# Durations and landing times of loads and crossbar transposes in a build-time instruction scheduler, changed

## The chip, the cores and the metric

The kernel runs on one core of one Trainium2 chip. The metric is the device time of one execution in microseconds (us). Every execution quoted here was in the fast state, with a granted TensorE clock of 0.993 to 1.000 of full speed. Ratios are the mean time of one kernel's fast runs over that of the other's of the same rounds, so they are not quite the ratios of the medians quoted beside them; intervals are 95%.

## The reference

Causal attention for 8 batches of 8 heads, 576 tokens of width 64, with 16 "beacon" keys and values in front that every token may see; then a two-layer MLP (512 to 2048 to 512) with a squared ReLU over all 4,608 tokens.

```python
k_all = np.concatenate([beacon_k, k], axis=2)          # B=8, H=8, 16+576, 64
v_all = np.concatenate([beacon_v, v], axis=2)
scores = scale * np.matmul(q, k_all.transpose(0, 1, 3, 2))
scores = np.where(causal, -1e9, scores)
a = softmax(scores)                                     # cut
x = np.matmul(a, v_all).transpose(0, 2, 1, 3).reshape(4608, 512)
r = np.maximum(x @ w_in, 0.0)
return (r * r) @ w_out
```

## The kernel before

The program is not written in its final order. The Python code adds some 1,360 operations, each with a guessed duration, a priority and what it depends on; a small event simulation ("the model") then plays them, and each engine's instructions are emitted in the order in which the model started them. The model's clock is never on the chip: what is frozen into the program is only the order. On the chip each engine takes its instructions in that order and waits, by semaphore, for whatever is not ready.

All DMAs share one modelled stream, `dma_free`; each adds its `dma` to it:

```python
# Order.run(): an operation starts on engine e at model time `now`
end = now + dur
free[e] = end
if op.dma:
    dma_free = max(dma_free, now + self.DMA_LAT[e]) + op.dma
    seen = max(end, dma_free + 1.6)          # model time at which its users may start
    lanes[e].append(seen)
    ...
else:
    seen = end + self.LAT[e]
```

The three kinds of DMA that the change touches:

```python
# add_load(): 128 rows of q, k or v of one batch, fp32, into a staging buffer; POOL casts it to bf16
ld = add(f"ld{b}{x}{c}", "POOL" if soft else "SP", 1.3 if lo else 0.65, emit_load, prio=prio, take=("stg", "stg"),
         dma=(1.15 if b < NPE else 1.25) * rows / 128, behind=load_chain[-1:] + behind, sync=sync)

# add_trans(): DMA transpose of a whole batch's q or k into qT or kT (batches 2 to 7; TensorE does batches 0 and 1)
trans[b, x] = [add(f"tr{b}{x}", "SP", 4.1, emit, prio=prio, deps=deps, dma=4.5)]

# add_first_loads(): the first 240 tokens of batch 0: head pair 0, pair 1, pairs 2-3; k on SP's queue, q on ACT's
for lo, hi in ((0, 1), (1, 2), (2, HP)):
    for n, (x, t) in enumerate((("k", k), ("q", q))):
        ... # emit: dma_start on (nc.sync, nc.scalar)[n]
        o = add(f"fld{x}{lo}", ("SP", "ACT")[n], (0.45, 0.55)[n], emit, prio=-300.0 + lo, dma=0.68 * (hi - lo))
```

In the middle of the run TensorE has two kinds of work to mix: attention of batch b, which needs loads and transposes that arrive by DMA, and MLP matmuls of earlier tokens, which need nothing from DMA. A good order puts attention where its data has landed and MLP everywhere else.

The softmax here doesn't subtract the row's maximum and nothing guards it: scores larger than these inputs give would overflow.

## Time and profile before

The median is 346.06 us at first (346.27 with the run taken beside the changed kernel). From the page of the profile of the kernel before, the span, PE's (TensorE's) line of the busy times, and the busy tenths of PE and DMA in 40 slices of 8.6 us:

```profile
span 345.0 us, 7128 instructions
...
PE 327.1 (95%) x2829; PEld 174.0 (50%) x2868; DVE 168.4 (49%) x372; ACT 194.7 (56%) x297; POOL 90.7 (26%) x141
...
PE   2799899999998999999999999999999999999995
...
DMA  9999969999999999998699979984014011011002
```

TensorE bounds the kernel: it is busy 95% of the span. DMA is nearly full until about 230 us and then hardly used: in that time attention's data arrives, and from 260 us on there is MLP work alone. (39 matmul records are missing from this trace: 2829 of 2868.)

What TensorE waited for in the kernel before (the view of waits: who waited for whom, then us in total, times, longest us; the view leaves out the shortest gaps, its smallest entries are 0.2 us):

```profile
PE ps L451 <- DVE qk_area L299: 6.4, 3, 4.0
PE ps L639 <- POOL vb L299: 2.9, 4, 1.2
PE strip L589 <- ACT pt L604: 1.0, 4, 0.4
...
PE strip L589 <- DVE kT L299: 0.5, 1, 0.5
```

The first line is the startup. The second is the attention's second product, which waits for casts of v; the last two times are these, in PE's timeline (start us, us, engine, line, operation, tiles, shape, count, and in brackets the idle time before it and what ended it):

```profile
107.34 0.45 PE L639 MATMUL ps<-vb,pt 128*128 128x65 bf16 x9
108.35 0.31 PE L639 MATMUL ps<-vb,pt 128*128 128x65 bf16 x5 [0.57 <-POOL vb L299]
109.44 0.19 PE L639 MATMUL ps<-vb,pt 80*128 80x65 bf16 x1 [0.78 <-POOL vb L299]
109.69 0.59 PE L770 MATMUL ps<-xT,w_in 128*128 128x512 bf16 x2
```

MLP matmuls (L770) were ready but stood behind it in the order. Last, VectorE (DVE) in the startup of the kernel before:

```profile
4.86 0.41 DVE L299 COPY kT<-ps 128x240 bf16<-128x240 bf16 x1
6.16 0.32 DVE L299 CAST qk_area<-osb 120x256 bf16<-120x256 f32 x1 [0.89 <-DMA osb<-in_k_dram]
6.40 0.17 DVE L299 COPY kT<-ps 128x64 bf16<-128x64 bf16 x1
7.16 0.41 DVE L299 COPY kT<-ps 128x240 bf16<-128x240 bf16 x1 [0.58 <-PE ps L451]
7.76 0.63 DVE L299 CAST qk_area<-osb 120x256 bf16<-120x256 f32 x2 [0.20 <-DMA osb<-in_q_dram]
8.75 0.42 DVE L614 TENSOR_TENSOR pt<-pt,tri 128x512 bf16<-128x512 bf16 x1 [0.36 <-ACT pt L604]
9.10 0.87 DVE L299 CAST qk_area<-osb 120x256 bf16<-120x256 f32 x2
```

The cast at 6.16 waits for head pair 1's k, and the beacon copy at 6.40, which the very first scores need, stands behind it.

### The profile page before, as it was taken

To read this page: it belongs to the slowest core of one execution; us is meant where nothing else is said; L and a number is where in the kernel's file an instruction comes from. 1 tells how busy PE (TensorE), PEld (TensorE's weight loads), DVE (VectorE), ACT (ScalarE), POOL (GpSimd) and SP (SyncE) were. 2 spreads that over 40 slices of the span, in tenths; PEclk is the share of its full clock that TensorE was granted. 3 is DMA by queue.
4 is the path that set the end of the run, shared out by engine and by line. 5 is a ranking of instruction groups with operands and counts; after the bars stand their busy time and mean duration, and the time that the engine had idled before them with its cause. 6 is when DMAs were issued, how large, how long until landed. Compare 5 with 4: busy or idle time off the path is not lost.

```text
span 345.0 us, 7128 instructions
## 1 busy us (share of the span) xinstructions
PE 327.1 (95%) x2829; PEld 174.0 (50%) x2868; DVE 168.4 (49%) x372; ACT 194.7 (56%) x297; POOL 90.7 (26%) x141
## 2 busy tenths in 40 slices
PE   2799899999998999999999999999999999999995
PEld 1567675544553444444456855544554444444442
DVE  5888884158534873575355546457533302401400
ACT  4796674377645764576656655577536416515611
POOL 9844703316414504250153115312000000000000
PEclk9999999999999999999999999999999999999999
DMA  9999969999999999998699979984014011011002
GB/s 169 220 206 220 205 101 209 214 240 211 177 219 198 232 182 170 209 221 176 142 256 207 178 148 208 228 204 101 2 64 128 0 61 63 0 61 64 0 21 101
DMA packets 145291, 51.88 MB, mean 150 GB/s; under 512 B 132458, under 2 KB 140010, under 8 KB 145258
## 3 DMA queue, kind: packets, MB, share of 16 engines
q1 hardware_dynamic: 135741, 42.45, 61.4%
q0 software_dynamic: 8512, 8.49, 14.5%
q10 hardware_dynamic: 1005, 0.49, 0.6%
q8 instruction: 22, 0.36, 0.5%
q14 instruction: 11, 0.09, 0.1%
HBM read 37.22 MB, written 9.44 MB: 135 GB/s over the span
## 4 chain that ended last, share of the span: by engine, by line
PE 78%; DMA 11%; SPq 3%; ACT 3%; POOL 2%; issue 1%; DVE 1%; DVEq 0%; ACTq 0%; POOLq 0%
PE ps L805 32%; PE ps L770 31%; PE ps L639 7%; DMA stg<-in_v_dram 6%; PE strip L589 6%; ACT pt L604 2%; DMA stg<-in_k_dram 2%; DMA stg<-in_q_dram 1%; DMA osb<-in_k_dram 1%; SPq L344 1%; SPq L376 1%; POOL vb L299 1%; POOL qk_area L299 1%; PE ps L451 1%; PE ps L707 0%
## 5 line engine op out<-in xcount | busy, mean ns | idle before, releaser
L770 PE MATMUL ps<-xT,w_in 128*128 128x512 bf16 (+3 forms) x690 | 133.2, 340 | 0.6
L805 PE MATMUL ps<-w_out,g 128*128 128x512 bf16 x551 | 131.2, 379 | 1.9 <-issue 0.8
L604 ACT ACTIVATE pt<-strip 128x832 bf16<-128x832 f32 (+4 forms) x128 | 103.6, 867 | 38.4 <-PE strip L589 38.2
L786 ACT ACTIVATE g<-ps 128x512 bf16<-128x512 f32 (+2 forms) x128 | 72.0, 562 | 47.9 <-PE ps L770 47.4
L770 PEld LDWEIGHTS <-w_in 128*128 128x128 bf16 x704 | 65.2, 98 | 57.6 <-issue 6.5
L795 DVE TENSOR_TENSOR g<-g 128x1024 bf16<-128x1024 bf16 (+2 forms) x80 | 52.4, 659 | 76.5 <-ACT g L786 75.3
L805 PEld LDWEIGHTS <-g 128*128 128x128 bf16 x576 | 52.5, 98 | 60.0 <-issue 3.2
L299 POOL CAST qk_area<-stg 128x512 bf16<-128x512 f32 (+2 forms) x60 | 39.3, 662 | 53.2 <-DMA stg<-in_k_dram 31.8
L299 POOL CAST vb<-stg 128x512 bf16<-128x512 f32 (+1 forms) x38 | 26.2, 697 | 87.4 <-DMA stg<-in_v_dram 83.0
L297 ACT COPY osb<-ps 128x512 f32<-128x512 f32 x26 | 15.2, 586 | 50.8 <-PE ps L805 44.5
L639 PEld LDWEIGHTS <-pt 128*128 128x128 bf16 (+1 forms) x960 | 36.4, 98 | 14.7 <-issue 3.4
L639 PE MATMUL ps<-vb,pt 128*128 128x65 bf16 (+1 forms) x960 | 40.3, 194 | 3.0 <-POOL vb L299 2.9
L589 PE MATMUL strip<-qT,kT 64*128 64x80 bf16 (+7 forms) x400 | 36.0, 283 | 2.2 <-ACT pt L604 1.0
L659 DVE TENSOR_TENSOR xn<-ps,rcp 128x320 bf16<-128x320 f32 (+2 forms) x64 | 31.5, 492 | 2.4 <-DVE rcp L657 0.2
L614 DVE TENSOR_TENSOR pt<-pt,tri 128x1024 bf16<-128x1024 bf16 (+1 forms) x36 | 23.6, 656 | 13.4 <-ACT pt L604 13.4
L657 DVE RECIPROCAL rcp<-ps 128x5 f32<-128x5 f32 (+2 forms) x64 | 12.3, 192 | 34.6 <-PE ps L639 34.4
L788 DVE TENSOR_SCALAR g<-ps 128x512 bf16<-128x512 f32 (+2 forms) x32 | 19.1, 599 | 9.9 <-PE ps L770 9.2
L589 PEld LDWEIGHTS <-kT 64*128 64x128 bf16 x400 | 12.8, 95 | 21.6 <-issue 17.0
L299 DVE COPY osb<-ps 128x512 f32<-128x512 f32 x10 | 6.9, 692 | 14.9 <-PE ps L805 14.6
L618 DVE TENSOR_TENSOR pt<-pt,tri 80x160 bf16<-80x160 bf16 x32 | 11.5, 359 | 0.0
L344 POOL DMA_DIRECT2D stg<-in_v_dram x10 | 8.5, 854 | 6.9 <-DMA w_in<-in_moe_w_in_dram 5.5
L451 PE MATMUL ps<-ident,qk_area 120*128 120x120 bf16 x16 | 2.5, 299 | 6.5 <-DVE qk_area L299 6.4
(39 smaller groups left out, 68.6 us busy)
## 6 DMA issues: line engine op xcount, KB each, us to landing
out_dram<-osb SPq DMA_DIRECT2D x17, 512.0 KB, 3.7
stg<-in_q_dram SPq DMA_DIRECT2D x24, 256.0 KB, 4.9
stg<-in_k_dram SPq DMA_DIRECT2D x18, 256.0 KB, 5.2
stg<-in_v_dram SPq DMA_DIRECT2D x18, 256.0 KB, 4.7
w_in<-in_moe_w_in_dram POOLq DMA_DIRECT2D x4, 512.0 KB, 11.1
w_out<-in_moe_w_out_dram POOLq DMA_DIRECT2D x4, 512.0 KB, 11.6
stg<-in_v_dram POOLq DMA_DIRECT2D x6, 256.0 KB, 8.4
stg<-in_k_dram SPq DMA_DIRECT2D x6, 224.0 KB, 4.2
```

Of the source, the lines that this page charges most:

```text
L297: nc.scalar.copy(dst, src)
L299: eng[e].tensor_copy(dst, src)
L589: nc.tensor.matmul(st[:, hj, at:at + t1 - t0], kT[b % 2][hp, pr, 128 * c:128 * c + 128], qT[b % 2][hp, pr, t0:t1], start=True, stop=True,)
L604: nc.scalar.activation(pt[take_pt.held[2]][:, :, off:off + width], st[:, :, 0:width], AF.Exp, bias=0.0, scale=scale)
L614: nc.vector.tensor_tensor(out=d, in0=d, in1=tri[:, m0:m0 + m, :][:, None].to_broadcast([128, 2, m, 128]), op=ALU.min)
L639: nc.tensor.matmul(a[:, at + (t - tl[0]) * (D + 1):at + (t - tl[0] + 1) * (D + 1)], P[0:rr, hj, o:o + 128], vb[b % 2][0:rr, c, 2 * pr + hj ...
L659: nc.vector.tensor_tensor(out=xn[b % 2].rearrange("p t (h d) -> p h t d", d=D)[:, h0:h0 + nh, tl[0]:tl[0] + nt], in0=a[:, :, :, 0:D], in1= ...
L770: nc.tensor.matmul(h[:, lo - spans[0][0]:hi - spans[0][0]], w_in_sb[:, mc, ft * 128:(ft + 1) * 128], xT[:, mc, lo % RING:lo % RING + hi - lo],
L786: nc.scalar.activation(dst, h, AF.Relu, bias=0.0, scale=1.0)
L788: nc.vector.tensor_scalar(out=dst, in0=h, scalar1=0.0, scalar2=None, op0=ALU.max)
L795: nc.vector.tensor_tensor(out=d, in0=d, in1=d, op=ALU.mult)
L805: nc.tensor.matmul(o, G[:, fc, ts * 128:(ts + 1) * 128], w_out_sb[:, fc, :], start=(fc == 0), stop=(fc == NFT - 1))
```

## The change

Its likely intent is to give the model what a trace shows: the first loads in their real landing order, v loads and crossbar transposes seen later than the stream alone would say, transposes that hold the stream for 3.7 us instead of 4.5, and batch 1's beacon keys out of the startup. No operation is added or removed; a few copies and casts come out on another engine (ACT has 6 instructions fewer, DVE 5 and POOL 1 more), as the model gives them to whichever engine is free.

```diff
-                 gate=None, dma=0.0, pe_time=0.0, behind=(), sync=()):
+                 gate=None, dma=0.0, pe_time=0.0, behind=(), sync=(), late=0.0):
@@ Order.run
                         lanes[e].append(seen)
+                        seen += op.late
@@ add_load
-                 prio=prio, take=("stg", "stg"), dma=(1.15 if b < NPE else 1.25) * rows / 128, behind=..., sync=sync)
+                 prio=prio, take=("stg", "stg"), dma=(1.15 if b < NPE else 1.25) * rows / 128, behind=..., sync=sync,
+                 late=0.0 if x != "v" or b == 0 else 1.0 if b < NPE else 2.0)
@@ add_trans
-        trans[b, x] = [add(f"tr{b}{x}", "SP", 4.1, emit, prio=prio, deps=deps, dma=4.5)]
+        trans[b, x] = [add(f"tr{b}{x}", "SP", 4.1, emit, prio=prio, deps=deps, dma=3.7, late=2.0)]
@@ add_beacon
+        if b:
+            bk.need.extend(norm_ops[HP - 1, 0])
@@ add_part_loads
-                        sync=() if pr or n else sync, deps=free, dma=1.07 if b == 0 else 1.5)
+                        sync=() if pr or n else sync, deps=free, dma=0.95 if b == 0 else 1.5)
@@ add_first_loads
-                o = add(f"fld{x}{lo}", ..., dma=0.68 * (hi - lo))
+                o = add(f"fld{x}{lo}", ..., dma={"k": (0.1, 1.7, 0.4), "q": (0.8, 0.5, 1.45)}[x][min(lo, 2)])
```

(cuts marked `...`; the bookkeeping of the new field is left out)

More of the change, by code (lines that the diff above doesn't have):

```diff
@@ L21 @@
                  "take", "give", "gate", "held", "slots", "dma", "pe_time", "behind", "followers",
-                 "sync", "insts")
+                 "sync", "insts", "late")
     def __init__(self, name, engs, dur, emit, prio=0.0, deps=(), take=None, give=None,
-                 gate=None, dma=0.0, pe_time=0.0, behind=(), sync=()):
+                 gate=None, dma=0.0, pe_time=0.0, behind=(), sync=(), late=0.0):
         self.name = name
+        self.late = late
         self.engs = engs if isinstance(engs, (tuple, list)) else (engs,)
@@ L348, in add_load @@
         ld = add(f"ld{b}{x}{c}", "POOL" if soft else "SP", 1.3 if lo else 0.65, emit_load,
-                 prio=prio, take=("stg", "stg"), dma=(1.15 if b < NPE else 1.25) * rows / 128, behind=load_chain[-1:] + behind, sync=sync)
+                 prio=prio, take=("stg", "stg"), dma=(1.15 if b < NPE else 1.25) * rows / 128, behind=load_chain[-1:] + behind, sync=sync,
+                 late=0.0 if x != "v" or b == 0 else 1.0 if b < NPE else 2.0)
         load_chain.append(ld)
@@ L489, in emit @@
                         in_=t[0, h, t0:t0 + np_ * ns, :].rearrange("h (p s) d -> p h s d", s=ns))]
-                o = add(f"fld{x}{lo}", ("SP", "ACT")[n], (0.45, 0.55)[n], emit, prio=-300.0 + lo, dma=0.68 * (hi - lo))
+                o = add(f"fld{x}{lo}", ("SP", "ACT")[n], (0.45, 0.55)[n], emit, prio=-300.0 + lo, dma={"k": (0.1, 1.7, 0.4), "q": (0.8, 0.5, 1.45)}[x][min(lo, 2)])
                 first.append(o)
```

## The prediction

> **What bounds the kernel now.** TensorE: the page gives PE 327.1 us busy of a 345.0 us span, at full granted clock in all 40 slices. PE time that no matmul explains sits in few places (PE's timeline, gaps over 0.25 us add up to 16 us): 4.0 us before the first matmul, about 7.5 us of stalls between 4 and 20 us, 1.36 us at 40 us, 0.5 at 81 us, 1.7 at 107.6 to 109.4 us, and 4.0 us of tail. From 110 to 340 us PE is practically full. So this change can win only in the startup and in three waits for v casts.
>
> **What it does.** No instruction is added or removed; the build-time scheduler gets other durations, and the in-order streams come out in another order.
>
> 1. First loads. The Trainium skill (Trainium Kernel Development and Optimization, Key Constraints) says that DMAs of different queues share the 16 DMA engines and interleave; the trace agrees: q pair 1 lands at 4.57 us, k pair 1, issued 0.25 us later, at 6.14, q pairs 2-3 at 7.74, k pairs 2-3 at 8.14. With its origin at 0.8 us, the old model has 5.14, 5.82, 7.18, 8.54; the new one 4.5, 6.2, 7.65, 8.05. On DVE, the 0.17 us beacon copy into kT (at 6.40, behind the k pair 1 cast that waited 0.89 us for its load) should move ahead of that cast, so the first scores matmul starts near 5.9 instead of 7.05; and the k casts of pairs 2-3 (from 9.10, behind a mask that itself idled 0.36 us) should come at 8.2, after their landing. ACT then starts exponentials about 1 us earlier; ACT is the limit until 25 us (5.00 of 5 us busy in 15 to 20), so 0.7 to 1.3 us survives.
> 2. Batch 1's beacon cast (0.72 us on DVE at 10.96) and its transposes (0.27 us on PE at 13.30) leave the startup. DVE idles 1.07 us soon after, so this is worth 0 to 0.5 us.
> 3. v loads of batch 1 taken 1 us later. At 40 us PE waits 1.20 us for the last v cast, which sits behind 1.04 us of zeroing on POOL though its load landed at 39.21. MLP stage 1 work is available: about 0.8 us.
> 4. v loads of later batches 2 us later: the waits at 81 and 107 to 109 us (2.1 us together, last v of batch 3 landing at 108.65) should be filled with MLP matmuls: about 1 us.
> 5. Transposes: 4.5 us to 3.7 of queue time but 2.0 later; the trace has 5.0 to 6.6 us from issue to landing. Only 0.4 us is waited on them, so nothing direct.
>
> **Sum.** 1.0 + 0.2 + 0.8 + 1.0 = 3 us. Predicted 343.2 us, 8 in 10 within 341.0 to 345.4. Faster by over 2%: 0.03; within 2%: 0.96; slower by over 2%: 0.01.
>
> **What would show it.** Right: PE's waits on POOL's v casts (2.9 us now) fall below 1 us; first scores matmul near 6 us; first MLP matmul at about 23.2 instead of 24.3 us; the tail and the 110 to 340 us stretch unchanged. Step 1 is wrong if the first MLP matmul stays at 24.3; step 4 if the gaps at 80 and 107 us persist or reappear elsewhere.
>
> **What would make it wrong.** The loads of 28 to 110 us are paced by DMA (about 200 GB/s), so PE work moved earlier may meet the same landings and the startup gain be given back as waits for v or weights; attention moved later may leave too little MLP work beside it; a reordered exponential or evacuation can open a new wait on PE.

## The result, and the profile after

The changed kernel took 350.19 us (median of 4, 348.77 to 351.07) against 346.27 us (345.67 to 346.60): ratio 1.0111, 1.0074 to 1.0148. It is slower by 1.1%, outside the predicted range and on the other side of no change.

The same lines of the page after:

```profile
span 348.5 us, 7165 instructions
...
PE 330.6 (95%) x2868; PEld 175.2 (50%) x2868; DVE 171.0 (49%) x377; ACT 191.5 (55%) x291; POOL 89.0 (26%) x142
...
PE   2889899999989999999999999999999999999995
...
DMA  8999969999999999999699959992014011011002
```

They tell almost nothing: PE is busy 95% again. Its busy time even rose by 3.5 us, but that compares a trace with all 2868 matmul records with one that lacks 39 (the counts of instructions differ mostly by these, too). The waits of TensorE after are more telling:

```profile
PE ps L456 <- DVE qk_area L301: 5.0, 3, 3.9
PE ps L644 <- POOL vb L301: 3.1, 7, 0.8
PE strip L594 <- ACT qT L299: 2.0, 3, 0.9
PE strip L594 <- DMA kT<-qk_area: 1.7, 2, 1.0
PE ps L712 <- DVE xn L664: 1.1, 3, 0.7
PE ps L644 <- ACT g L791: 0.4, 1, 0.4
```

The waits for v casts (vb) did not fall from 2.9 us, they came seven times instead of four; and scores matmuls now wait for a transpose to land (kT, 1.7 us), which none did for more than a trifle before.

**Where the time went.** To place it, take the start of each weight load (these records are complete), subtract the nominal time of all matmuls ordered before it (nominal from the traces: 0.865 us for four 512-column matmuls, 0.0305 us for one of the attention's second product, and so on), and call the rest TensorE's lag: the time it has lost so far. Its absolute size depends on the nominal times chosen; the differences between two kernels hardly do.

| lag of TensorE, us, at | 10 us | 20 us | 30 us | 50 us | 90 us | 120 us | 200 us | 220 us | 260 us | 340 us |
|---|---|---|---|---|---|---|---|---|---|---|
| before | 8.4 | 12.2 | 12.9 | 14.6 | 16.1 | 18.4 | 20.7 | 21.6 | 22.3 | 22.3 |
| after | 8.3 | 12.2 | 13.0 | 14.7 | 16.3 | 19.4 | 22.1 | 23.4 | 26.0 | 25.8 |

Up to 90 us there is no difference: the startup won nothing and the wait at 40 us is still there. The 3.5 us are lost between 90 and 260 us, and nothing happens in the pure MLP part. The prediction had called 110 to 340 us "practically full" and foretold no change there; most of the loss lies in that stretch. Listing the places where a group of matmuls took longer than nominal gives almost all of it (the scores of every batch show 0.3 us against my nominal time in both kernels, so the differences count):

| place | before, us | after, us | waits for |
|---|---|---|---|
| second product, batch 2, 81 us | 0.66 | 1.18 | last v cast |
| first scores, batch 3, 98 us | 0.31 | 1.21 | kT transpose |
| second product, batch 3, 108 us | 1.65 | 0.94 | last v casts |
| second product, batch 4, 135 us | under 0.2 | 0.48 | v cast |
| second product, batch 6, 200 us | under 0.2 | 0.73 | v cast |
| first scores, batch 7, 224 us | 0.31 | 1.10 | kT transpose |
| second product, batch 7, 233 us | 0.36 | 1.27 | v casts |

The differences add up to about 3.5 us. PE's timeline after shows the last two:

```profile
224.44 0.63 PE L644 MATMUL ps<-vb,pt 128*128 128x65 bf16 x15
225.79 0.58 PE L594 MATMUL strip<-qT,kT 64*128 64x496 bf16 x4 [0.72 <-DMA kT<-qk_area]
226.30 2.76 PE L775 MATMUL ps<-xT,w_in 128*128 128x512 bf16 x12
...
232.87 0.44 PE L644 MATMUL ps<-vb,pt 128*128 128x65 bf16 x9
233.70 0.31 PE L644 MATMUL ps<-vb,pt 128*128 128x65 bf16 x5 [0.39 <-ACT g L791]
234.27 0.19 PE L644 MATMUL ps<-vb,pt 80*128 80x65 bf16 x1 [0.26 <-POOL vb L301]
```

At 225.79 twelve MLP matmuls that came next in the order were not let past. The Trainium skill (TensorE: Matmul & The Clock Gate, "Step-by-step: what each phase is for") says that only weight loads are pulled ahead and matmuls stay in program order; the trace agrees, with 0.72 us idle in front of work that ran at once afterwards. In the before kernel, the place that does the same scores reads:

```profile
225.72 2.75 PE L770 MATMUL ps<-xT,w_in 128*128 128x512 bf16 x12
228.41 0.58 PE L589 MATMUL strip<-qT,kT 64*128 64x496 bf16 x4
```

The chain of what ended last, after, shows what that kT transpose itself stood on (start us, us, what): loads, a cast, the transpose.

```profile
208.32 5.14 DMA stg<-in_q_dram
...
213.85 6.17 DMA stg<-in_k_dram
...
220.14 0.62 POOL qk_area L301
...
220.78 4.97 DMA kT<-qk_area
225.74 0.05 issue
225.79 0.58 PE strip L594 x4
```

The same transpose in the kernel before (its issue in SP's timeline, and the time to landing in the view of tile kT for 220 to 222 us):

```profile
220.80 3.68 SPq L376 DMA_TRANSPOSE kT<-qk_area  x1
DMA to landing us min/median/max: 5.0/5.0/5.0
```

This transpose did not get slower. **In both traces it is issued at 220.8 us and has landed at 225.7 or 225.8 us.** The change only moved the matmuls that need it: from 2.6 us after the landing to the landing itself. At batch 3 that is only about half of the lost slack: its kT was issued at 93.5 and 93.3 us, but landed at 99.2 us before and at 100.1 after. Slack, computed as the time at which TensorE was ready for the batch's first scores (their start less the loss in the table above) less the landing of kT, was +0.8 us for batch 3 and +2.3 for batch 7 before; after, it is -1.2 and -1.1. These are single executions: in the nine traces with transposes at 4.5 us or less, the last kT landed anywhere from 222.7 to 226.3 us.

**Why the order moved.** Set the model's issue of this last transpose (plus 0.8 us, the trace's own start) against the trace: before 223.9 us against 220.8, so the model was 3.1 us behind the chip; after 217.3 against 220.8, so the model runs 3.5 us ahead of it. By stretch, from the issue of batch 2's first k load to the last transpose:

| sum over the batches, us | before: model | trace | after: model | trace |
|---|---|---|---|---|
| first k load to qT transpose (loading and casting k and q) | 83.5 | 87.0 | 77.4 | 83.3 |
| qT transpose to kT transpose | 26.4 | 24.7 | 26.3 | 24.6 |
| kT transpose to the next batch's first k load (v, stores) | 63.6 | 59.8 | 64.3 | 62.8 |

Loading k and q takes longer on the chip than in the model, by 3.5 us in sum before and by 5.9 after; the other two stretches take less. Taking 0.8 us off each transpose shortened the model in the first line (83.5 to 77.4 us), as the next loads queue behind the transposes in the one modelled stream. (Which line takes up a change is a matter of the order, too: with only the transposes at 5.2 us it is the third, 78.0 us in the model.) Before, the errors more than cancelled: 173.5 us in the model, 171.5 in the trace. After, they don't: 168.0 against 170.7. The transposes were corrected and the loads were not. That is the theory to test; as 3.7 us agrees with one reading of the trace (SP is held for 3.70 us by the median qT transpose; what a transpose takes of the DMA engines, beside loads in packets of the same 256 bytes, the trace does not separate), it says that a better number may have been put in and the sum became false.

### The profile page after: what moved, and what is told of

It is laid out like the page before. It is cut to its first block, busy times and chain, and to the rows that moved or that the text cites. A ratio compares the mean times of both kernels' runs of the same rounds, so it can differ in the third digit from the quotient of the medians.

```text
span 348.5 us, 7165 instructions
## 1 busy us (share of the span) xinstructions
PE 330.6 (95%) x2868; PEld 175.2 (50%) x2868; DVE 171.0 (49%) x377; ACT 191.5 (55%) x291; POOL 89.0 (26%) x142
## 4 chain that ended last, share of the span: by engine, by line
PE 62%; DMA 23%; SPq 7%; POOL 4%; issue 1%; DVE 0%; POOLq 0%; ACT 0%; ACTq 0%
PE ps L775 27%; PE ps L810 27%; DMA stg<-in_k_dram 7%; DMA stg<-in_v_dram 7%; DMA stg<-in_q_dram 4%; PE ps L644 4%; PE strip L594 4%; DMA w_in<-in_moe_w_in_dram 4%; SPq L379 2%; SPq L346 2%; SPq L695 2%; POOL vb L301 1%; DMA kT<-qk_area 1%; POOL qk_area L301 1%; SPq L345 1%
## 5 line engine op out<-in xcount | busy, mean ns | idle before, releaser
L775 PE MATMUL ps<-xT,w_in 128*128 128x512 bf16 (+3 forms) x704 | 134.9, 341 | 0.2 <-DVE qT L301 0.2
L810 PE MATMUL ps<-w_out,g 128*128 128x512 bf16 x576 | 134.3, 379 | 0.0
L791 ACT ACTIVATE g<-ps 128x512 bf16<-128x512 f32 (+2 forms) x122 | 68.3, 560 | 45.2 <-PE ps L775 44.5
L800 DVE TENSOR_TENSOR g<-g 128x1024 bf16<-128x1024 bf16 (+2 forms) x80 | 53.7, 672 | 70.9 <-ACT g L791 69.0
L301 POOL CAST qk_area<-stg 128x512 bf16<-128x512 f32 (+2 forms) x60 | 38.3, 644 | 67.2 <-DMA stg<-in_k_dram 45.5
L299 ACT COPY osb<-ps 128x512 f32<-128x512 f32 x25 | 14.7, 586 | 58.4 <-PE ps L810 57.7
L644 PE MATMUL ps<-vb,pt 128*128 128x65 bf16 (+1 forms) x960 | 41.2, 194 | 3.6 <-POOL vb L301 3.1
L793 DVE TENSOR_SCALAR g<-ps 128x512 bf16<-128x512 f32 (+2 forms) x38 | 23.2, 613 | 15.0 <-PE ps L775 14.6
L619 DVE TENSOR_TENSOR pt<-pt,tri 128x1024 bf16<-128x1024 bf16 (+1 forms) x36 | 23.2, 645 | 8.6 <-ACT pt L609 8.5
L594 PEld LDWEIGHTS <-kT 64*128 64x128 bf16 x400 | 12.7, 95 | 22.0 <-issue 14.2
L301 DVE COPY osb<-ps 128x512 f32<-128x512 f32 x11 | 7.6, 692 | 15.1 <-PE ps L810 14.7
L623 DVE TENSOR_TENSOR pt<-pt,tri 80x160 bf16<-80x160 bf16 x32 | 9.8, 307 | 0.0
## 6 DMA issues: line engine op xcount, KB each, us to landing
stg<-in_k_dram SPq DMA_DIRECT2D x6, 224.0 KB, 3.8
```

The costliest lines, as they stand in the source:

```text
L301: eng[e].tensor_copy(dst, src)
L594: nc.tensor.matmul(st[:, hj, at:at + t1 - t0], kT[b % 2][hp, pr, 128 * c:128 * c + 128], qT[b % 2][hp, pr, t0:t1], start=True, stop=True,)
L619: nc.vector.tensor_tensor(out=d, in0=d, in1=tri[:, m0:m0 + m, :][:, None].to_broadcast([128, 2, m, 128]), op=ALU.min)
L644: nc.tensor.matmul(a[:, at + (t - tl[0]) * (D + 1):at + (t - tl[0] + 1) * (D + 1)], P[0:rr, hj, o:o + 128], vb[b % 2][0:rr, c, 2 * pr + hj ...
L775: nc.tensor.matmul(h[:, lo - spans[0][0]:hi - spans[0][0]], w_in_sb[:, mc, ft * 128:(ft + 1) * 128], xT[:, mc, lo % RING:lo % RING + hi - lo],
L791: nc.scalar.activation(dst, h, AF.Relu, bias=0.0, scale=1.0)
```

## The experiments

All outputs were correct. Each kernel ran 6 times (in five rounds and a profile). The four kernels of one block ran on one chip and share its 11 runs of the kernel before.

### Block 1: the parts of the change

Theory 1: the transposes' 3.7 us alone. Theory 2: the lateness terms. Theory 3: the new startup. The kernel before took 346.64 us (345.52 to 348.03).

**Only the 3.7 us undone** (from the changed kernel):

```diff
-  tr{b}{x} ... dma=3.7, late=2.0
+  tr{b}{x} ... dma=4.5, late=2.0
```

> The changed kernel with only the crossbar transposes' queue time put back from 3.7 to 4.5 us. Theory 1 (the 3.7 us makes the model's load stream run ahead of the chip's, so TensorE meets loads and transposes that have not landed): at least 3 of the 3.9 us lost come back, 346.0 to 347.0 us, and the last kT transpose is issued in the trace no later than the model has it. Theory 2 (the lateness terms hurt, by pushing attention and stores about): stays at 349 to 351 us. Theory 3 (the new startup hurts): stays at 349 to 351 us.

Measured 345.90 us (345.30 to 347.71), ratio 0.9990 (0.9961 to 1.0020). The whole loss is gone, slightly under the range of theory 1. The model is again behind the trace at the last transpose: 223.7 against 220.5 us. Its profiled execution, at 347.63 us one of its two slowest, has no wait for a transpose, but 3.3 us of waits for v casts, 1.5 of them at 111 us and 1.2 at 212 us; so the kernel can still be slow in single executions.

**Only the 3.7 us done** (from the kernel before):

```diff
-  tr{b}{x} ... dma=4.5
+  tr{b}{x} ... dma=3.7
```

> The kernel before with only the transposes' queue time set to 3.7 us. Theory 1: loses most of it by itself, 348.5 to 351 us, with the model ahead of the trace by 2 to 4 us at the last transposes. Theories 2 and 3: 346 to 346.8 us, as before.

Measured 350.65 us (349.73 to 351.05), ratio 1.0108 (1.0082 to 1.0134): this number alone makes the whole loss. The model is ahead of the trace by 2.1 us. TensorE's waits and, below, its timeline at batch 3's first scores, which in the kernel before (last of these three fences) needed no wait:

```profile
PE strip L591 <- DMA kT<-qk_area: 2.3, 1, 2.3
PE ps L641 <- POOL vb L301: 1.6, 3, 1.2
```

```profile
96.78 1.03 PE L807 MATMUL ps<-w_out,g 128*128 128x512 bf16 x4
100.13 0.98 PE L591 MATMUL strip<-qT,kT 64*128 64x496 bf16 x4 [2.33 <-DMA kT<-qk_area]
```

```profile
99.81 0.51 PE L639 MATMUL ps<-vb,pt 128*128 128x65 bf16 x11
100.25 0.58 PE L589 MATMUL strip<-qT,kT 64*128 64x496 bf16 x4
```

The scores start at 100.1 and 100.3 us, so at nearly the same time in both; kT had landed at 100.1 us with the 3.7 us and at 99.2 us in the kernel before. So 0.9 us of the wait is a later landing in this execution; the rest is that TensorE has less to do before the scores: it idles before them in the one and works up to them in the other. At this transpose, where over half of the loss falls, the model is level with the trace (0.1 us ahead, where the kernel before is 1.3 us behind): the lead at the last transpose is a summary, not the place of the loss.

**Only the lateness terms** (v loads 1.0 and 2.0 us, transposes 2.0 us):

```diff
+  ld{b}v{c} ... late=0.0 if b == 0 else 1.0 if b < NPE else 2.0
-  tr{b}{x} ... dma=4.5
+  tr{b}{x} ... dma=4.5, late=2.0
```

> The kernel before with only the lateness terms (v loads 1 or 2 us, transposes 2 us). Theory 1: 345.0 to 346.8 us, and TensorE's wait for the v cast of batch 3 near 108 us is smaller. Theory 2: 349 to 351 us.

Measured 345.62 us (344.81 to 346.79), ratio 0.9972 (0.9947 to 0.9997). Theory 2 falls: lateness helps a little. Its profile has no wait of TensorE for a v cast at all.

**Only the startup parts** (first loads, part loads 0.95, batch 1's beacon cast behind the norms):

```diff
+  bk.need.extend(norm_ops[HP - 1, 0])                      # b > 0
-  sld0... dma=1.07        fld... dma=0.68 * (hi - lo)
+  sld0... dma=0.95        fld... dma={"k": (0.1, 1.7, 0.4), "q": (0.8, 0.5, 1.45)}
```

> The kernel before with only the startup parts (first loads' order, part loads 0.95 us, batch 1's beacon cast behind batch 0's norms). Theory 1: 345.5 to 347.0 us, since after 25 us TensorE's accumulated idle time was the same in both kernels although the first scores matmul came 1.7 us and the first MLP matmul 1.2 us earlier. Theory 3: 349 to 351 us.

Measured 346.93 us (346.36 to 347.27), ratio 1.0008 (0.9986 to 1.0030). Theory 3 falls too, and so does my own claim of about 1 us from the startup. (Its trace has two waits of 0.4 us for a kT transpose: waits of that size do not show in the time.)

### Block 2: is it the transposes or the pace of the stream?

The kernel before took 345.36 us (344.34 to 347.55) on this chip.

**3.7 us kept, k and q loads charged more** (from the changed kernel):

```diff
-  dma=(1.15 if b < NPE else 1.25) * rows / 128
+  dma=(1.15 if b < NPE else 1.25 if x == "v" else 1.38) * rows / 128
```

> The changed kernel, transposes still at 3.7 us, but the k and q loads of batches 2 to 7 taken as 1.38 us instead of 1.25 per 128 rows, which puts the modelled issue of the last kT transpose at 224.0 us as in the kernel before (223.1). If what matters is the pace of the whole modelled stream, wherever the time is charged (theory 1): 345.0 to 347.0 us. If the transposes themselves must be charged 4.5 us: stays at 349 to 351 us.

Measured 345.45 us (344.61 to 346.60), ratio 0.9991 (0.9956 to 1.0025). The loss is gone with the transposes still at 3.7 us. So the transposes need not be charged 4.5 us: the pace of the whole modelled stream matters, and here it did not matter where the time was charged.

**Transposes at 4.1 us** (from the changed kernel):

```diff
-  tr{b}{x} ... dma=3.7, late=2.0
+  tr{b}{x} ... dma=4.1, late=2.0
```

> The changed kernel with the transposes at 4.1 us; the model issues the last kT transpose at 218.5 us, against 216.5 of the change and 220 to 221 us that every trace so far shows. Theory 1: in between, 346.5 to 349.5 us, with some waits for transposes or v casts left.

Measured 348.59 us (346.43 to 350.77), ratio 1.0076 (1.0031 to 1.0122): in between, as expected. Its spread of 4.3 us is the widest of all. The profile fell on its fastest execution (346.43), where the model was 2.4 us behind the trace at the last transpose and 0.1 us at batch 3's. Whether that margin was too small in its other executions is not shown, as none of them was traced.

**Only the v lateness** (from the kernel before):

```diff
+  ld{b}v{c} ... late=0.0 if b == 0 else 1.0 if b < NPE else 2.0
```

> The kernel before with only the v loads' lateness (not the transposes'). If the v lateness is what takes TensorE's waits for v casts away: 345.0 to 346.2 us, and these waits fall from about 2.9 us to below 1 us; the 8-in-10 range of my step 3 and 4 sum was 1.8 us.

Measured 345.73 us (344.05 to 347.52), ratio 0.9997 (0.9956 to 1.0038). TensorE's waits for v casts are down to 0.2 us in the profile, as expected, yet the mean time does not show it. The profiled execution was one of the faster ones (344.64), so its lag is no fair measure. This one stays inconclusive: a gain of up to 0.4% is not excluded. (The last clause of the expectation is badly put: 1.8 us was the sum of my steps 3 and 4, not a range.)

**Transposes at 5.2 us, otherwise the kernel before:**

```diff
-  tr{b}{x} ... dma=4.5
+  tr{b}{x} ... dma=5.2
```

> The kernel before with the transposes at 5.2 us: a model still slower than the chip, last kT transpose at 231.0 us in the model. If being late is cheap and being early dear: 345.0 to 347.0 us, no waits of TensorE for transposes. If any mismatch costs, by its size: 348 us or more.

Measured 344.56 us (344.19 to 345.38), ratio 0.9962 (0.9927 to 0.9998): a little under the range for "late is cheap". The further mistake in that direction is a gain. "Any mismatch costs by its size" falls.

### Block 3: a version that beats both, the other limit, and the startup

The kernel before took 345.51 us (344.34 to 346.96) on this chip.

**The whole change, with the transposes at 5.2 us:**

```diff
-  tr{b}{x} ... dma=3.7, late=2.0
+  tr{b}{x} ... dma=5.2, late=2.0
```

> The changed kernel with the transposes at 5.2 us: everything of the change kept, the modelled stream slower than the chip (last kT transpose at 231.4 us in the model). Theory 1 (early is dear, late is cheap): 343.5 to 346.0 us, no waits of TensorE for transposes, a narrow spread. A rival by which the lateness terms or the new startup cost anything by themselves would have it above the kernel before.

Measured 344.48 us (343.97 to 344.71), ratio 0.9962 (0.9940 to 0.9983). It beats both kernels, by 0.4% the one before. Three of its waits of TensorE; the first line is from 17 and 18 us, the second from 40 us, and of the third 0.3 us are at 105 us. What is left out is the startup and "issue" (1.0 us):

```profile
PE ps L712 <- DVE xn L664: 0.6, 2, 0.3
PE ps L644 <- POOL vb L301: 0.6, 1, 0.6
PE strip L594 <- ACT pt L609: 0.5, 2, 0.3
```

No scores matmul waits for a transpose; slack behind the kT landing is 2.8 us (batch 3) and 7.6 us (batch 7). It also spreads less: 0.7 us over 6 runs, while the kernel before spread over 2.6 us in its 11 runs on the same chip.

**v lateness and 5.2 us, without the new startup and the transposes' lateness:**

```diff
+  ld{b}v{c} ... late=0.0 if b == 0 else 1.0 if b < NPE else 2.0
-  tr{b}{x} ... dma=4.5
+  tr{b}{x} ... dma=5.2
```

> The kernel before with the v loads' lateness and the transposes at 5.2 us, without the new startup and the transposes' lateness: the two parts that did best alone. If their gains add: 343.5 to 345.0 us, 0.3 to 0.7 per cent under the kernel before; candidate for the fastest version.

Measured 344.49 us (344.30 to 345.13), ratio 0.9967 (0.9944 to 0.9990). The same as the last one: 5.2 us brings nearly all of it, and the gain of v lateness does not add to it visibly, probably because both take away the same waits: with 5.2 us alone, one wait for a v cast is left (1.2 us, at 40 us).

**The whole change, with the transposes at 6.0 us:**

```diff
-  tr{b}{x} ... dma=3.7, late=2.0
+  tr{b}{x} ... dma=6.0, late=2.0
```

> As the first run of this call, with the transposes at 6.0 us (last kT transpose at 240.4 us in the model, some 20 us behind what the chip has shown). If being late never costs: same as at 5.2 us. If attention pushed too late leaves the MLP short of tokens: slower than at 5.2 us by 0.5 to 2 us, with new waits of TensorE in the middle of the run, for xT or g and not for loads.

Measured 345.20 us (344.92 to 346.09), ratio 0.9990 (0.9968 to 1.0013): 0.7 us above the run at 5.2, and its fastest execution (344.92) is slower than the slowest of that one (344.71). Being late does cost in the end. The new wait after 30 us is for the attention's normalized output (xn, 0.8 us at 104 us, where 5.2 us had none), not for xT or g, which I had named.

**First loads of pairs 2 and 3 split, on top of the 5.2 us version:**

```diff
-  for lo, hi in ((0, 1), (1, 2), (2, HP)):
+  for lo, hi in ((0, 1), (1, 2), (2, 3), (3, HP)):
-  dma={"k": (0.1, 1.7, 0.4), "q": (0.8, 0.5, 1.45)}[x][min(lo, 2)]
+  dma={"k": (0.1, 1.7, 0.2, 0.2), "q": (0.8, 0.5, 0.75, 0.7)}[x][lo]
```

> As the first run of this call, with the first loads of pairs 2 and 3 split into one load per pair. If TensorE's start is gated by landings, which is why the earlier first scores matmul gained nothing: the transposes of pair 2 start at 8.3 to 8.8 us instead of 9.1 and TensorE's accumulated idle time at 10 us is 0.3 to 0.6 us lower; the total moves by less than 0.5 us. If something else gates it (the engines' order): pair 2's transposes stay near 9.1 us.

Measured 345.37 us (344.18 to 346.25), ratio 0.9987 (0.9961 to 1.0013). Pair 2's k landed at 6.66 us instead of 7.61 and its transposes on TensorE started at 7.35 instead of 8.25 us (the unsplit version already had 8.25, so the comparison with 9.1 in the expectation was with the wrong kernel). So that start is gated by the landing. But SP issued the fourth load only at 3.95 us, it landed at 10.18, and pair 3's transposes slid from 8.53 to 10.59 us. TensorE's lag at 10 us fell from 8.0 to 7.4 us and at 20 us rose from 11.1 to 12.7. The idea as such was a miss: the total is 0.9 us above the unsplit version, where the expectation was less than 0.5 us either way.

### All together

Model issue of the last kT transpose (plus 0.8 us) against the trace; a positive last column means that the model runs ahead of the chip.

| kernel | transposes' `dma` | ratio to before | model, us | trace, us | model ahead by |
|---|---|---|---|---|---|
| the change | 3.7 | 1.0111 | 217.3 | 220.8 | +3.5 |
| only 3.7 | 3.7 | 1.0108 | 217.8 | 219.9 | +2.1 |
| change at 4.1 | 4.1 | 1.0076 | 219.3 | 216.9 | -2.4 |
| only startup | 4.5 | 1.0008 | 222.6 | 220.0 | -2.7 |
| before | 4.5 | 1 | 223.9 | 220.8 | -3.1 |
| change, 3.7 undone | 4.5 | 0.9990 | 223.7 | 220.5 | -3.2 |
| only lateness | 4.5 | 0.9972 | 224.9 | 221.4 | -3.5 |
| v lateness and 5.2 | 5.2 | 0.9967 | 231.8 | 226.9 | -5.0 |
| only v lateness | 4.5 | 0.9997 | 224.0 | 218.7 | -5.4 |
| only 5.2 | 5.2 | 0.9962 | 231.8 | 225.6 | -6.2 |
| change, k and q loads 1.38 | 3.7 | 0.9991 | 224.8 | 218.4 | -6.4 |
| change at 5.2, first loads split | 5.2 | 0.9987 | 232.5 | 226.0 | -6.5 |
| change at 5.2 | 5.2 | 0.9962 | 232.2 | 224.0 | -8.1 |
| change at 6.0 | 6.0 | 0.9990 | 241.2 | 231.4 | -9.8 |

The two kernels whose model is ahead are the two slowest; the change at 4.1 us, the least behind of all, is the third. That any new order loses by chance is an unlikely rival: the ten other new orders are 2.7 us or more behind, and none of them is measurably slower than the kernel before. Among these ten the margin does not order the ratios (-5.4 gives 0.9997, -3.5 gives 0.9972). The trace's column is one execution of each kernel.

## Why the prediction was wrong, point by point

**Step 5 is the one that failed.** It said of the transposes "Only 0.4 us is waited on them, so nothing direct". I asked what TensorE waited for in the old order and took its absence for slack. But the old order had next to no such wait because its matmuls came after the landings, by 0.8 us at batch 3 and 2.3 at batch 7, with the model 1.3 and 3.1 us behind the chip there, and the same line of the diff took 0.8 us away for each of twelve transposes. All of the 1.1% is in that number: alone it gives 1.0108, undone it gives 0.9990. The one part of the diff that I costed at zero was the whole result. The general risk was named ("PE work moved earlier may meet the same landings"), but of the startup, not of the stream, and its size was not computed, though the model's arithmetic (12 times 0.8 us at most; the model's last transpose in fact moved by 6.6 us, against a margin of 3.1 that could be read from the trace) was there to do. In place of "nothing direct", the runs show a loss of about 4 us, with TensorE waiting 1.0 and 0.7 us for kT in the changed kernel, beside more and later waits for v casts, and 2.3 us for kT in the one with the 3.7 us alone. That all of the 4 us come from the stream's pace is inferred from the two runs that undo the loss in different places of the stream.

**Step 1, the first loads: mechanism seen, size wrong.** The first scores matmul moved from 7.05 to 5.66 us (5.9 predicted; the 1.7 us in an expectation above was read from its first weight load, at 5.36) and the first MLP matmul from 24.32 to 23.15 us (23.2 predicted). VectorE after:

```profile
4.80 0.51 DVE L301 COPY kT<-ps 128x240 bf16<-128x240 bf16 x2
6.03 0.42 DVE L301 CAST qk_area<-osb 120x256 bf16<-120x256 f32 x1 [0.72 <-DMA osb<-in_k_dram]
7.13 0.41 DVE L301 COPY kT<-ps 128x240 bf16<-128x240 bf16 x1 [0.67 <-PE ps L456]
7.76 0.43 DVE L301 CAST qk_area<-osb 120x256 bf16<-120x256 f32 x1 [0.23 <-DMA osb<-in_q_dram]
8.45 0.82 DVE L301 CAST qk_area<-osb 120x256 bf16<-120x256 f32 x2 [0.25 <-DMA osb<-in_k_dram]
```

The beacon copy now comes before the waiting cast, exactly as foretold. But that cast still waits for the same load, and the second pair's scores start 1.45 to 1.58 us after the landing of its k in 12 of 14 traces, old startup or new (7.62 us before, 7.59 after). So TensorE's lag at 20 us is 12.2 us in both. Both events that I named as proof of the gain happened, and there was no gain in the pair: the first MLP matmuls had been put in front of batch 0's last attention, which ended later (its last second product started at 28.39 instead of 26.64 us). Over all unsplit traces the lag at 30 us averages 13.5 us with the old startup (six) and 12.9 with the new (seven), so some 0.5 us may be real; the timing, 1.0008 with 0.9986 to 1.0030, does not resolve it. My ground for 0.7 to 1.3 us, that ACT is the limit until 25 us, is not borne out: after the change ACT was busy 4.89 of 5 us in 15 to 20 us and 4.22 in 20 to 25, against 5.00 and 4.88 before.

**Step 2, batch 1's beacon cast: not separated.** It was only run together with step 1; the two give nothing that the clock shows.

**Step 3, the wait at 40 us: not won in the changed kernel.** That place lost 1.49 us before and 1.36 after, as this execution's last v of batch 1 landed at 40.09 us instead of 39.21. Over the traces, TensorE lost on average 1.1 us between 30 and 50 us with v lateness (nine traces, the split one left out) and 1.7 without (four). So 0.8 us was about right in size, and smaller than the differences between executions.

**Step 4, later v loads: right alone, undone in company.** With lateness alone, the waits for v casts go from 2.9 us to 0.2 or to none. In the change they were 3.1 us. That the lateness was eaten by a stream that ran ahead fits the changed kernel, but does not explain it all: with the stream's pace restored (3.7 undone) they were still 3.3 us in the profiled execution, with k and q loads at 1.38 they were 0.8. Why is open.

**The range.** I gave 0.01 to slower by over 2% and was right not to expect that, but the range 341.0 to 345.4 left no room for any loss. A change that only reorders can lose, too: this one lost 1.1%, and with one number different (5.2 us) it won 0.4%. The range should have reached well past no change.

**What stays open.** Why the change at 4.1 us is slow although its profiled execution kept a margin of 2.4 us: later landings in its other executions would explain it, but only the fastest was profiled. What sets the spread of landings between executions was not found.

## What to carry to other kernels

If a build-time model freezes the order of in-order engines, an error that makes it later than the chip can cost little (here the fastest versions were 5 to 8 us behind at the last transpose, though others as far behind won nothing, and at 10 us it began to cost), while one that makes it earlier can be dear (here about 4 us for 2.1 and 3.5 us ahead). This is one kernel, bound by TensorE. So set its times for the late side of what executions show, not for one trace, and check the accumulated model time against the trace at several points whenever one duration is corrected, since two wrong numbers may be holding each other up. And when "nobody waits for X" is read from a profile, ask how much slack there is behind X before calling a change to it free: idle time says what the wait is, landing against use says what it will become.

## What the Trainium skill lacked or had wrong

- DMA: Bandwidth & Descriptors ("Latency and other measured facts") gives 261 GB/s for a DMA transpose with a non-contiguous middle dimension, measured on one kernel. Here one transpose of 128 x 2560 bf16 (655,360 bytes) held SP for 3.0 to 4.6 us (qT, kernel before; median 3.7), and took 4.9 to 7.8 us from issue to landing (q and k; the prediction's 5.0 to 6.6 was too narrow), beside other loads. An estimate from the median, 655,360 bytes over 3.7 us, is 177 GB/s. That does not show the page wrong: its kernel's layout is not shown to be this one's, and the time that SP is held need not be the transfer's. What it lacks is the time of a transpose beside other loads.
- No page that I found says by how much landings vary between executions. The second k load of this kernel, issued at 1.73 to 1.75 us, landed anywhere from 5.31 to 6.97 us in fourteen traces of fourteen orders that were near alike up to there; whole executions of the kernel before spread over 3.7 us on the chips used.
- TensorE: Matmul & The Clock Gate ("Step-by-step: what each phase is for") states that matmuls stay in program order; nothing contradicted it. What no page adds is the consequence measured here: a transpose that landed at the same time in both kernels (225.8 and 225.7 us) cost nothing with its user 2.6 us later and 0.72 us of idle TensorE with its user on top of it.
